# Regrouping a product inside SBUF by small transfers, and moving table building to GpSimd

## Chip, cores and metric

One core of one Trainium2 chip. The time is the device time of one execution in microseconds (us). Every kernel was also executed once under the profiler, and all spans, durations and waits below are from that execution. A time is some 2 us longer than the span of the same execution.

Engines are named as in the profile: PE is TensorE (PEld its weight loads), DVE VectorE, ACT ScalarE, POOL GpSimd, SP SyncE. Here SP only issues transfers.

## The reference, cut to what matters

```python
# A: S = 2048 positions, D = 640 channels
k_shift = sum over t < 4 of k_pad[:, t:t + S, :] * shift_k[:, 3 - t]   # short conv, 4 taps
kv = k_shift * v
y  = irfft(rfft(kv, 2 * S) * rfft(ssm_k, 2 * S))[:S] + kv * ssm_D      # long conv
x  = x + ga * (h * y)                    # h = modulated layernorm of x
# B: gMLP
z  = gelu(h2 @ w_in);  z1, z2 = halves of z
x  = x + gb * ((z1 * (w_sp @ layernorm(z2) + b_sp)) @ w_out)
```

The modulation rows (sa, ca, ga, sb, cb, gb) are silu(c) @ w_mod.

## The kernel before

The long convolution is done as matrix products with cosine tables (M2 forward, G2 inverse), in five units of 128 channels. The operations of part A are recorded with a planned cost and a wish for their time. A planner then takes them one by one, so it fixes the order on each engine, and where it expects PE to stand idle it puts in filler matmuls of the identity. Each engine works its list strictly in order.

The transform wants kv with (8 channels x 16 blocks) on the 128 partitions; the short conv leaves it with one channel to a partition. The kernel before goes through DRAM: one write and one read per unit, 512 KB each.

```python
# tables: "turns" and their rounding; t is the label that the plan orders by
def turns(e):
    new(a, "T", [P, 2, KCH, P], F32)
    for h in range(2):
        e.tensor_scalar(tl[a][:, h], tl["mbase"][:], mstep[:, h * NCH + i:h * NCH + i + 1], MAGIC, op0=ALU.add, op1=ALU.add)
op({"DVE": 540, "POOL": 1000}, turns, ...)
op({"DVE": 650}, lambda e: e.scalar_tensor_tensor(tl[a][:], tl[a][:], MAGIC, ...))   # rounding
# ... Sin on ACT follows

# short conv of unit dt
op({"DVE": 650} if dt == 0 else {"DVE": 650, "POOL": 1050}, diag, ...)    # dg = identity x taps
#   4 times: taps (4 matmuls into PSUM), then times_v: product over v, in place in "big"
op(dma(512, 300), lambda e: e.dma_start(kv_scr[dt * P:(dt + 1) * P, :], tl[name][:, KPAD + S:]), ...)

# per unit, before its first stage: the read
load_X("XU%d" % u, kv_fft, u, ("XU%d" % u, 0), [("kvs", u)])
# kv_fft = kv_scr.rearrange("(c g) (n f) -> (g n) c f", g=8, f=P)
```

## Time and profile before

| kernel before | value | how to read it |
|---|---|---|
| time | 355.31 us | median of 3 runs, 350.15 to 355.49 |
| span | 350.2 us | profiled execution, mean granted clock 0.985 |
| busy | PE 95%, DVE 63%, ACT 40%, POOL 26% | fillers count as busy |
| HBM | read 16.11 MB, written 5.24 MB | includes 5 writes and 5 reads of kv |
| first "pz" (inverse transform) | 52.0 us | end of the ramp |
| first z matmul | 163.0 us | start of part B |

In the profile lines, big holds k and v of a unit and then its product, X the regrouped product or filter, dg the diagonals, T and ZTp the tables of turns, wm a piece of w_mod, Z the result of the inverse transform and ZT its transposed copy; s, sm, pu and pz are results of PE in PSUM.

All later runs of this kernel lie between 350.1 and 355.9 us on one continuous spread. Runs over 1.5% above its fastest count as slow and are left out of the ratios.

One queue of this kernel matters later and is not among the lines that the prediction shows: SP's own timeline (start, duration, queue, line, operation, out<-in). These are the loads of k for units 1 and 2:

```profile
25.71 4.63 SPq L642 DMA_TRANSPOSE big<-in_A_k_dram  x1
...
32.37 1.98 SPq L642 DMA_TRANSPOSE big<-in_A_k_dram  x1
```

Both are issued by 34.4 us, though the product of unit 1 is only written at 45.64 us. In this order SP runs well ahead of need.

### The profile page before, as it was taken

The numbers are of one execution on the slowest core, as the hardware profiler recorded it, in microseconds if no ns is written. First come the engines' busy times: TensorE is split into PE (matmuls) and PEld (weight loads), VectorE is DVE, ScalarE is ACT, GpSimd is POOL, SyncE is SP. The second block draws the span as 40 slices with busy tenths as digits, with TensorE's granted clock in tenths as the row PEclk, the third lists the DMA queues.
The fourth block names the chain that finished last, engine by engine and source line by source line (L and its number), as shares of the span: only waits on it lengthen the run. The fifth ranks groups of instructions, "written<-read, shape, count | busy, mean of one in ns | idle before, by whom it ended". The sixth has DMA issues, their size and how long they took to land.

```text
span 350.2 us, 6998 instructions
## 1 busy us (share of the span) xinstructions
PE 332.2 (95%) x2923; PEld 213.2 (61%) x2929; DVE 219.9 (63%) x465; ACT 139.2 (40%) x225; POOL 89.8 (26%) x101
## 2 busy tenths in 40 slices
PE   8578899999999999998999999999999999999996
PEld 3236458786877988874555555555555555555554
DVE  6887999995857999789787867723223322332323
ACT  2358847878766785536555555200000000000000
POOL 1000310586894796261310023900000000000000
PEclk9789999999999999989999999999999999999999
DMA  7769777993959296430330696057545455631111
GB/s 118 213 194 204 195 206 194 197 250 23 232 89 309 44 249 178 131 97 3 75 75 2 121 216 168 0 113 149 122 107 105 112 126 119 129 87 47 45 45 58
DMA packets 128343, 45.04 MB, mean 129 GB/s; under 512 B 117592, under 2 KB 127672, under 8 KB 128312
## 3 DMA queue, kind: packets, MB, share of 16 engines
q1 hardware_dynamic: 127008, 44.59, 56.4%
q8 instruction: 23, 0.38, 0.4%
q10 hardware_dynamic: 1304, 0.00, 0.2%
q14 instruction: 8, 0.07, 0.1%
HBM read 16.11 MB, written 5.24 MB: 61 GB/s over the span
## 4 chain that ended last, share of the span: by engine, by line
PE 83%; DVE 8%; ACT 5%; issue 2%; POOL 1%; ACTq 0%; DVEq 0%; POOLq 0%
PE ps L1031 27%; PE pz L384 18%; PE pu L384 17%; PE po L1049 9%; PE sm L384 7%; PE s L384 4%; ACT X L406 2%; ACT KH L406 1%; DVE st L692 1%; DVE T L605 1%; DVE st L847 1%; ACT Z L957 1%; DVE T L510 1%; DVE dg L654 1%; DVE T L508 0%
## 5 line engine op out<-in xcount | busy, mean ns | idle before, releaser
L1031 PE MATMUL ps<-X,wT 128*128 128x432 bf16 x512 | 95.7, 346 | 0.0
L1031 PEld LDWEIGHTS <-wT 128*128 128x128 bf16 x512 | 50.1, 98 | 42.2
L605 DVE TENSOR_TENSOR T<-pu,KH 128x1024 bf16<-128x1024 f32 x40 | 47.7, 1218 | 8.1 <-PE pu L384 4.9
L1042 ACT COPY uT<-pt 128x896 bf16<-128x896 bf16 x1 | 0.9, 905 | 118.9 <-PE pt L1041 118.9
L384 PEld LDWEIGHTS <-Z 128*128 128x128 bf16 x320 | 31.2, 98 | 27.4 <-ACT Z L957 0.4
L384 PE MATMUL pu<-X,M 128*128 128x128 bf16 (+1 forms) x480 | 45.4, 237 | 1.1 <-DVE T L605 0.6
L406 ACT CAST X<-s 128x1024 bf16<-128x1024 f32 x40 | 40.9, 1022 | 10.9 <-PE s L384 10.8
L384 PE MATMUL pz<-T,G 128*128 128x128 bf16 (+1 forms) x480 | 41.5, 237 | 0.0
L384 PEld LDWEIGHTS <-M 128*128 128x128 bf16 x480 | 35.8, 98 | 7.3 <-issue 1.3
L1034 DVE SCALAR_TENSOR_TENSOR u<-ps,bcol,G 128x432 bf16<-128x432 f32 x18 | 12.0, 668 | 42.2 <-PE ps L1031 42.2
L384 PEld LDWEIGHTS <-G 128*128 128x128 bf16 x480 | 34.7, 98 | 3.1
L384 PE MATMUL pu<-big,Z 128*128 128x432 bf16 x160 | 33.1, 346 | 0.0
L1049 PE MATMUL po<-w_o,uT 128*128 128x320 bf16 (+1 forms) x224 | 32.8, 299 | 0.0
L384 PE MATMUL pz<-big,Z 128*128 128x432 bf16 x160 | 32.8, 346 | 0.0
L406 ACT CAST Z<-pz 128x512 bf16<-128x512 f32 x40 | 23.5, 592 | 16.8 <-PE pz L384 16.8
L1034 DVE SCALAR_TENSOR_TENSOR u<-ps,bcol,M 128x432 bf16<-128x432 f32 x14 | 9.3, 667 | 30.0 <-PE ps L1031 29.9
L1049 PEld LDWEIGHTS <-uT 128*128 128x128 bf16 (+1 forms) x224 | 21.8, 98 | 9.8
L771 POOL TENSOR_TENSOR gh<-gh,gca_bf 128x512 bf16<-128x512 bf16 x20 | 22.5, 1153 | 18.2 <-DVE gca_bf L758 13.1
L406 ACT CAST KH<-pu 128x512 bf16<-128x512 f32 x40 | 22.7, 600 | 5.9 <-PE pu L384 5.4
L771 POOL TENSOR_TENSOR gh<-gh,gsa_bf 128x512 bf16<-128x512 bf16 x20 | 22.5, 1154 | 7.1 <-DVE gsa_bf L761 7.1
L1051 DVE TENSOR_TENSOR ot<-po,xt 128x320 bf16<-128x320 f32 x32 | 15.7, 492 | 13.4 <-PE po L1049 13.4
L988 DVE BATCH_NORM_STATS2 stz<-X 128x6 f32<-128x432 bf16 x32 | 18.8, 601 | 8.5 <-ACT X L982 8.2
(126 smaller groups left out, 361.0 us busy)
## 6 DMA issues: line engine op xcount, KB each, us to landing
wm<-in_w_mod_dram SPq DMA_DIRECT2D x6, 800.0 KB, 4.9
xt<-in_A_q_dram SPq DMA_DIRECT2D x4, 640.0 KB, 5.5
X<-in_A_ssm_k_dram SPq DMA_DIRECT2D x5, 512.0 KB, 8.0
kv_scr<-big SPq DMA_DIRECT2D x5, 512.0 KB, 3.1
X<-kv_scr SPq DMA_DIRECT2D x5, 512.0 KB, 5.7
out_dram<-ot SPq DMA_DIRECT2D x16, 160.0 KB, 2.2
big<-in_B_w_in_dram SPq DMA_DIRECT2D x2, 1080.0 KB, 6.0
w_o<-in_B_w_out_dram SPq DMA_DIRECT2D x6, 160.0 KB, 3.2
```

What stands on the lines that cost most here:

```text
L384: nc.tensor.matmul(o, lhsT=w, rhs=x, start=start, stop=stop)
L406: (e.copy if e is nc.scalar else e.tensor_copy)(dst, src)
L510: op({"DVE": 650}, lambda e: e.scalar_tensor_tensor(tl[a][:], tl[a][:], MAGIC, tl["mbase"][:, None].to_broadcast([P, 2, KCH, P]), op0=ALU. ...
L605: e.tensor_tensor(T_[:], tl[pu][:, :, :, None, :].to_broadcast([P, KP, 2, 2, DU]), tl[KH][:, :, None, :, :].to_broadcast([P, KP, 2, 2, DU] ...
L654: e.tensor_tensor(tl[dg][:], ident[:, None, :].to_broadcast([P, 4, P]), sk[:, dt, :, None].to_broadcast([P, 4, P]), op=ALU.mult)
L692: e.bn_stats(out=st[:, a, :], in_=xt[:, n, a * HS:(a + 1) * HS])
L771: lambda e, vec=vec, o=o: e.tensor_tensor(gvu, gvu, vec[:, None, d0:d0 + du].to_broadcast([P, TB, du]), op=o),
L988: op({"DVE": 620}, lambda e, i=i, n=n, fc=fc: e.bn_stats(out=stz[:, n, fc, :], in_=tl[z2][:, i, fc * FC:(fc + 1) * FC]), r=[(z2, (i, fc))] ...
L1031: nc.tensor.matmul(ps[:, :FC], lhsT=wTs[t][:, s_, :], rhs=tl["z2_%d" % (s_ // TB)][:, s_ % TB, fc * FC:(fc + 1) * FC], start=(s_ == 0), st ...
L1034: nc.vector.scalar_tensor_tensor(u[:, sl], ps[:, :FC], bcol[:, t:t + 1], z1[t][:, sl], op0=ALU.add, op1=ALU.mult)
L1049: nc.tensor.matmul(ps[:, :HS], lhsT=uTs[t][:fsz[ft], ft, :], rhs=w_o[:fsz[ft], ft, h * HS:(h + 1) * HS], start=(ft == 0), stop=(ft == NFT ...
L1051: nc.vector.tensor_tensor(ot[:, h * HS:(h + 1) * HS], ps[:, :HS], xt[:, t, h * HS:(h + 1) * HS], op=ALU.add)
```

## The change

The intent: drop the DRAM round trip (its latency and its HBM traffic) by 16 transfers per unit from SBUF to SBUF; take the table building off DVE, which is busy in the ramp; load the Sin table of ACT at the start. The planner's wishes were searched again, so the order changed everywhere.

```diff
+        def turn_kv(u):
+            def fn(e):
+                X = new(name, "X", [P, DU // 8, P])
+                for i in range(DU // 8):
+                    e.dma_start(X[:, i, :], tl[kv][i * 8:(i + 1) * 8, KPAD + S:].rearrange("g (n f) -> g n f", f=P))
+            op({"SP": 3700}, fn, ...)
-            op(dma(512, 300), lambda e: e.dma_start(kv_scr[...], tl[name][:, KPAD + S:]), ...)
-            load_X("XU%d" % u, kv_fft, u, ...)
+            turn_kv(u)
-            op({"DVE": 540, "POOL": 1000}, turns, ...)
+            op({"POOL": 1000}, turns, ...)                  # two instructions
-            op({"DVE": 650} if dt == 0 else {"DVE": 650, "POOL": 1050}, diag, ...)
+            op({"POOL": 1050}, diag, ...)
-            op({"DVE": 350, "POOL": 1050}, <negation of a part of G2>)
+            op({"POOL": 1050}, <the same>)
-            op({"DVE": 700}, <copy of a part of G2>)
+            op({"DVE": 700, "ACT": 1040}, <the same>, alt="gc")
+        nc.scalar.activation(warm[:], halfpi[:], ACT.Sin)   # early table load
# cut: f1 and e tables as planned operations, a few planned costs, LOOK 31 -> 94,
# and the tables of wishes WANT, SHIFT, SECOND (all numbers new)
```

On the engines: 16 turns, four diagonals and four negations leave DVE for POOL; six normalizations go from DVE to ACT, three copies of Z from ACT to DVE; 80 transfers stand in place of 10.

## The prediction

> **What bounds the kernel now.** I read the page first, then a table of stretches, then the order of events in the first 60 us, then the groups of the engines that the change touches. On the page I looked at the rows of slices (each slice is 8.75 us):
>
> ```profile
> PE   8578899999999999998999999999999999999996
> ...
> DVE  6887999995857999789787867723223322332323
> ...
> PEclk9789999999999999989999999999999999999999
> ```
>
> TensorE looks busy nearly everywhere, so I asked what it was busy with. The table of stretches gives, after each stretch, its length, then busy us and instruction count of PE, PEld, DVE, ACT and POOL, the granted clock, the DMA share and GB/s:
>
> ```profile
> 10.00:20.00 10.00, 6.55 (x19) 2.35 (x18) 7.76 (x18) 2.72 (x6) 0.00 (x0) 0.66 0.53 140
> 20.00:30.00 10.00, 6.68 (x69) 3.50 (x68) 7.86 (x25) 7.64 (x13) 0.11 (x1) 1.00 1.11 238
> 30.00:40.00 10.00, 9.08 (x110) 6.37 (x108) 9.69 (x28) 9.65 (x16) 0.83 (x2) 1.00 1.08 242
> 40.00:50.00 10.00, 9.66 (x76) 4.59 (x77) 9.12 (x19) 4.87 (x7) 1.87 (x3) 1.00 0.46 151
> 60.00:150.00 90.00, 87.65 (x1243) 73.41 (x1244) 72.19 (x106) 64.22 (x98) 60.24 (x57) 1.00 0.78 169
> ```
>
> Nineteen matmuls in 10 us, then 69, then 110, against 1243 in 90 us later: the early "busy" is partly filler (matmuls of the identity that only keep the clock up) and partly matmuls at a low clock. Both instruction orders contain the same 2853 real matmuls in the recorded part; fillers fall from 76 to 68. So the work on TensorE does not change, and only its waste can. I sized it. By the chain's rows an uninterrupted forward group takes 0.44 us, an inverse group 0.88, a tap group 0.86, and the chain and groups give 0.40 for a first-stage group. 80 x 0.44 + 40 x 0.88 + 20 x 0.86 + 40 x 0.40 is 103.6 us; the modulation, flips and last stage add about 21, so some 124 us. The first z matmul starts at 163.0, after 3 fillers, and from there TensorE is never idle until 340. So about 38 us are waste before 162.5, and nothing after it can change.
>
> Where it lies: the first inverse matmul, "pz", starts at 52.00. Ahead of it in the order stand 12 tap groups, 12 first-stage groups, 12 forward groups, 32 flips and one modulation row: 10.3 + 4.8 + 5.3 + 1.8 + 0.7, about 23 us. So the ramp wastes 29 of the 38 us and the rest 9. The timeline shows why the ramp is slow (start, duration, engine, line, what):
>
> ```profile
> 3.60 1.28 ACT L424 ACT_TABLE_LOAD   x1 [3.60 <-DVE gmask L447]
> ...
> 8.36 1.29 DVE L654 TENSOR_TENSOR dg<-ident,sk 128x512 bf16<-128x512 bf16 x2
> ...
> 13.72 1.28 DVE L669 TENSOR_TENSOR big<-sm,big 128x512 bf16<-128x512 f32 x2
> 14.84 3.62 PE L384 MATMUL sm<-big,dg 128*128 128x512 bf16 x8
> 18.50 0.69 DVE L669 TENSOR_TENSOR big<-sm,big 128x512 bf16<-128x512 f32 x1 [1.01 <-PE sm L384]
> 19.21 0.34 SPq L672 DMA_DIRECT2D kv_scr<-big  x1
> 20.91 0.40 PE L384 MATMUL s<-F1bd,X 64*128 64x128 bf16 x8
> 22.30 0.37 SPq L545 DMA_DIRECT2D X<-kv_scr  x1
> ```
>
> VectorE builds tables first, makes the diagonals at 8.36 and table turns until 13.72; TensorE holds two tap results and waits. Its clock falls, the last two tap groups run at half speed, the product is finished at 19.19, and the kernel's transform starts at 20.91. The ACT copies between its four groups end at 29.7. The regrouped product would have landed at about 28.0 (22.30 plus the median 5.7), yet its first group runs at 31.65: the DRAM trip is mostly hidden behind VectorE and ACT.
>
> **What the Trainium skill says.** "TensorE: Matmul & The Clock Gate", Part 1, has a cold array at half the clock after an idle window of some 3.4 us. The trace agrees: the clock was 0.51 in 15 to 20 us and the two tap groups took 3.62 us instead of 1.72. "DMA: Bandwidth & Descriptors", § Why a DMA increments its semaphore by 16 and not by 1, has a copy use the largest number of engines up to 16 that divides both sides' slowest dimension; a transfer from 8 partitions to 128 would use 8. No run yet shows it. "SBUF — State Buffer", § Who interferes with whom, has a VectorE instruction with two SBUF inputs contend with a GpSimd instruction that reads SBUF; the table rounding that stays on VectorE is of that kind. The trace of before has no such pair close together in the ramp, so it does not say. "ScalarE: Activation LUTs", § What ACT_TABLE_LOAD costs, has about 1283 ns for a load; the row above has 1.28 us.
>
> **The change part by part.** These are the rows whose engine changes (busy us, mean ns; the first five are VectorE from 0 to 60 us):
>
> ```profile
> L669 DVE TENSOR_TENSOR big<-sm,big 128x512 bf16<-128x512 f32 x12 | 7.9, 678 | 2.9 <-PE sm L384 2.9
> ...
> L510 DVE SCALAR_TENSOR_TENSOR T<-T,ZTp 128x512 f32<-128x512 f32 x8 | 5.5, 691 | 0.2
> L508 DVE TENSOR_SCALAR T<-ZTp,mstep 128x256 f32<-128x256 f32 x16 | 4.9, 348 | 0.0
> ...
> L654 DVE TENSOR_TENSOR dg<-ident,sk 128x512 bf16<-128x512 bf16 x4 | 2.7, 684 | 0.0
> ...
> L535 DVE TENSOR_SCALAR G<-G 128x1024 bf16<-128x1024 bf16 x4 | 1.7, 427 | 0.1
> ...
> L654 POOL TENSOR_TENSOR dg<-ident,sk 128x512 bf16<-128x512 bf16 x1 | 1.0, 1040 | 6.8 <-PE sm L384 6.8
> ```
>
> VectorE loses 16 table turns (4.9 us), four diagonals (2.7) and four negations (1.7), all in the ramp, 9.3 us in sum; over the first part it also gives six normalizations of 0.44 to ACT (at 0.92 there) and takes three Z copies of about 0.6. GpSimd, 1.54 us busy in the first 10 us and idle in the next ten, takes 16 turns of about 0.45 (estimate, from 716 ns for its 640-element cast), five diagonals of 1.04 and four negations of about 1.
>
> The Sin table load moves to the start. It lay under VectorE work but held VectorE for 1.0 us before F1bd; gain about 1 us on the way to the first turn.
>
> Transfers: per unit one write and one read of 512 KB go away, 3.1 us and 5.7 us one after the other, 8.8 us. In their place stand 16 transfers of 32 KB. An issue took 338 to 367 ns for either old form, so 16 take about 5.4 us, and the last lands some 2 us later: about 7.4 us. Saved latency 1.4 us a unit; SP is 4.7 us longer in issues but no longer waits for the write to land. HBM loses 2.6 MB each way.
>
> The ramp after, by the new order: 31 fillers before the first tap instead of 22, nine more at about 0.22, so taps start near 10 us (before 9.11). GpSimd has the first four turn pairs at about 6.4 and the diagonal at 7.4, in time. VectorE ends its tables near 8, does four roundings (0.69) and four copies with sign (0.22), and meets the first tap result at about 12.0 instead of 13.72. Tensor idle time there is short, so I expect the clock to hold: four multiplications of 0.68 with tap groups between end at about 15.5, not 19.2. The kernel's transform starts near 15 instead of 20.91; ACT has four copies of 1.02 and eight Sins of 0.46 to do and ends near 22.5 instead of 29.7. The regrouped product lands near 15.5 + 7.4 = 23, just in time. ACT then has the two table loads (3.0), three copies, eight KH copies of 0.58 and three normalizations, to about 38. VectorE's list before the first spectral product is 16.5 us long (eight statistics of 1.1, copies, four multiplications) after about 19: 35.5. So the first "pz" stands at 37 without a stall; I add 3 us for stalls that such a reckoning misses: 40.
>
> In the new order 8 tap groups, 10 first-stage groups, 11 forward groups and the same flips and row stand before it: 6.9 + 4.0 + 4.8 + 2.5, 18.2 us. Its waste is 40 - 18.2 = 21.8 us against 29.0: 7.2 us saved. For the end of this part (9 fillers fall to 4, and gb's product moves ahead) I add 1 us; for the middle, 0. Sum 8.2 us.
>
> **The rivals.** First: the middle gives it back. Work starts earlier but VectorE (72.2 of 90 us), ACT and GpSimd (60.2) still have to serve it, and GpSimd's chain of modulations starts only when w_mod has arrived. For it: GpSimd was at 10.00 of 10 us in one stretch. Against: VectorE's total falls by over 9 us. It would leave 3 to 4 us, a time near 350. Second: GpSimd and VectorE block each other in the first 15 us, and small transfers on half of the engines take 10 us or more; then the product waits at 26 to 28 and the gain is some 4 us. Third: the transfers hardly matter and all of the gain is VectorE relief; this is compatible with my sum, for only 1.4 us of latency is in it. Fourth: the clock. If the longer filler and denser taps avoid every cold window, up to 2 us more come back.
>
> **Range and chances.** The profiled run took 352.19 us for a span of 350.2; the three timed runs average 353.65. Taking 8 to 9 us from these gives 344 to 345.4: I say 344.5. With no stalls (11 us) and a kept clock it is 339 to 341; with the first two rivals 349 to 351. So 339 to 350. Two per cent below the runs of before lies at 346 to 348, a little above my value: faster by over 2% has 0.64, within 2% 0.32, slower by over 2% 0.04.
>
> **What would show it.** Right: from the first z matmul on, the same length as before (187 us); first tap near 10; last multiplication of the first unit at 15 to 16 at full clock; first pz near 37 to 40; the DMA rows of kv_scr gone and 80 issues of about 0.34 us in their place. Wrong: a first pz after 45 (the ramp didn't shorten); a first pz at 38 but z matmuls still after 158 (the middle gave it back, and VectorE or GpSimd is then named in front of the pu and pz groups); low clock in 10 to 25 us; first-stage groups of the product waiting for DMA for over 2 us; roundings on VectorE that take well over 0.69 us beside GpSimd.

## The result and the profile after

The kernel after takes 366.0 us (median of 4 runs, 364.75 to 368.37), beside 353.56 us for the kernel before in the same comparison. The ratio is 1.039 (95% interval 1.028 to 1.051): slower. Ratios here compare fast runs alone, so they are not quite the ratio of the medians. All four runs are of the fast state. The profiled span is 363.0 us, the mean clock 0.972. HBM traffic fell as meant, to 13.49 MB read and 2.62 MB written.

The rows of slices on the page (9.1 us a slice), to set against those of before:

```profile
PE   8387998997999996996999999999999999999996
...
PEclk9977999999999999996899999999999999999999
```

The second slice of PE is a hole now (3, before 5), and the later slices show 7s and 6s where before had 9s. The table of stretches (length, then busy us and count of PE, PEld, DVE, ACT, POOL, then clock, DMA share, GB/s):

```profile
10.00:20.00 10.00, 4.13 (x16) 1.65 (x16) 7.18 (x12) 3.42 (x8) 8.41 (x9) 0.92 0.54 157
20.00:30.00 10.00, 7.24 (x52) 3.50 (x51) 7.94 (x12) 5.26 (x8) 8.29 (x8) 0.67 0.27 36
...
60.00:150.00 90.00, 82.33 (x1127) 66.45 (x1134) 64.17 (x95) 61.02 (x91) 56.87 (x52) 1.00 0.86 176
```

From 10 to 30 us DVE executes 24 instructions in place of 43, and POOL is busy 8.4 and 8.3 of 10 us. From 60 to 150 us PE executes 116 matmuls fewer than before at the same full clock (some records can be missing). So the loss has two places.

The first place, in the timeline (the bracket has the idle time ahead and what ended it):

```profile
2.67 9.01 POOL L502 TENSOR_SCALAR T<-ZTp,mstep 128x256 f32<-128x256 f32 x8 [0.53 <-DVE pj L428]
...
11.64 2.05 POOL L660 TENSOR_TENSOR dg<-ident,sk 128x512 bf16<-128x512 bf16 x2
...
11.72 3.72 DVE L504 SCALAR_TENSOR_TENSOR T<-T,ZTp 128x512 f32<-128x512 f32 x3 [3.92 <-POOL T L502]
...
12.74 1.90 PE L379 MATMUL sm<-big,dg 128*128 128x512 bf16 x8 [2.69 <-POOL dg L660]
```

Eight turns hold POOL for 9 us. The diagonals stand behind them in POOL's list, the first tap waits for a diagonal and starts at 12.74 us (before 9.1), and DVE waits 3.92 us for turns. The summary of single lines (ns: least, median, most) has the sizes:

```profile
L502 POOL TENSOR_SCALAR T<-ZTp,mstep x16: 1137/1148/1509, 2.7 to 23.2; 128x256 f32<-128x256 f32 x16
```

```profile
L504 DVE SCALAR_TENSOR_TENSOR T<-T,ZTp x8: 676/862/2518, 11.7 to 26.2; 128x512 f32<-128x512 f32 x8
```

```profile
L549 SPq DMA_DIRECT2D X<-big x80: 607/607/807, 21.5 to 133.5; - x80
```

A turn is 1.15 us on POOL, against 0.348 on DVE before. The rounding on DVE, 0.691 before, has a median of 0.86 and a longest of 2.52 us. That longest one, at 11.72, lies beside the two diagonals on POOL (11.64 to 13.69), not beside turns: where only turns overlap, roundings take 0.68 to 0.88, and in b_pool, where only the turns moved, 0.96 at most. And an issue of the new transfers is 0.607 us.

The second place, in SP's timeline:

```profile
21.55 10.78 SPq L549 DMA_DIRECT2D X<-big  x16
32.37 1.70 SPq L644 DMA_TRANSPOSE big<-in_A_k_dram  x1
...
45.60 10.41 SPq L549 DMA_DIRECT2D X<-big  x16
56.12 2.02 SPq L644 DMA_TRANSPOSE big<-in_A_k_dram  x1
```

The 16 issues hold SP for 10.4 to 10.8 us a unit, and the loads of k for units 1 and 2 leave only when they are over. PE's waits for transfers between 21 and 175 us (engine, tile and line, what was waited for: us in total, times, longest) are all new; the kernel before had none there:

```profile
PE s L379 <- DMA X<-big: 1.9, 3, 1.2
PE sm L379 <- DMA wm<-in_w_mod_dram: 1.6, 1, 1.6
PE sm L379 <- DMA ZT<-Z: 1.6, 1, 1.6
PE sm L379 <- DMA big<-in_A_k_dram: 1.3, 1, 1.3
```

To compare all kernels I cut each trace at the first pz and at the first z matmul, and reckon for the first two parts the waste: the time, less PE's real work in it at the durations of undisturbed groups. Ahead of the first z stand the same groups in every kernel, 123.4 us of work; 23.0 of it come before the first pz in the order of before and 18.3 in the new order. (Five of the traces lack records of six to nine tap matmuls; the work is counted with them.) Part B has the same work in each kernel, so its plain length stands there. All are profiled executions; an own reckoning, good to some half us.

| kernel | first tap | first pz | waste to first pz | waste first pz to first z | first z to end | span |
|---|---|---|---|---|---|---|
| before | 9.1 | 52.0 | 29.0 | 10.6 | 187.2 | 350.2 |
| after | 12.7 | 49.5 | 31.2 | 18.5 | 189.8 | 363.0 |
| a_both | 10.4 | 43.7 | 25.4 | 11.4 | 189.9 | 350.0 |
| a_turns | 10.3 | 43.9 | 25.6 | 18.9 | 189.5 | 357.4 |
| a_dram | 12.8 | 47.4 | 29.1 | 11.1 | 189.2 | 352.8 |
| b_sbuf | 9.1 | 52.3 | 29.3 | 11.7 | 187.3 | 351.7 |
| b_pool | 9.1 | 56.0 | 33.0 | 10.6 | 187.2 | 354.2 |
| a_hold | 10.3 | 43.9 | 25.6 | 23.0 | 189.0 | 361.0 |
| a_ahead | 10.9 | 43.1 | 24.8 | 17.1 | 189.7 | 355.0 |
| a_nopool | 10.3 | 44.2 | 25.9 | 11.7 | 189.4 | 350.4 |

### The profile page after: what moved, and what is told of

It is laid out like the page before. It is cut to its first block, busy times and chain, and to the rows that moved or that the text cites. A ratio compares the mean times of both kernels' runs of the same rounds, so it can differ in the third digit from the quotient of the medians.

```text
span 363.0 us, 7073 instructions
## 1 busy us (share of the span) xinstructions
PE 333.6 (92%) x2912; PEld 214.2 (59%) x2921; DVE 215.8 (59%) x437; ACT 143.7 (40%) x230; POOL 117.4 (32%) x125
## 3 DMA queue, kind: packets, MB, share of 16 engines
HBM read 13.49 MB, written 2.62 MB: 44 GB/s over the span
## 4 chain that ended last, share of the span: by engine, by line
PE 52%; DVE 6%; ACT 1%; POOL 1%; issue 0%; ACTq 0%; POOLq 0%
PE ps L1036 25%; PE pz L379 9%; PE po L1054 8%; PE pu L379 8%; DVE X L1002 2%; DVE st L851 1%; DVE T L609 1%; ACT Z L962 1%; DVE gh L834 0%; DVE gh L793 0%; POOL xt L845 0%; POOL rstdz L320 0%; PE sm L955 0%; PE pu L816 0%; ACT Z L932 0%
## 5 line engine op out<-in xcount | busy, mean ns | idle before, releaser
L1036 PEld LDWEIGHTS <-wT 128*128 128x128 bf16 x512 | 50.0, 98 | 43.7 <-issue 1.7
L379 PE MATMUL pu<-big,Z 128*128 128x432 bf16 x160 | 34.2, 353 | 0.0
L379 PE MATMUL pz<-big,Z 128*128 128x432 bf16 x160 | 33.6, 348 | 0.0
L401 ACT CAST Z<-pz 128x512 bf16<-128x512 f32 x37 | 21.6, 589 | 18.4 <-PE pz L379 18.4
L379 PE MATMUL sm<-big,dg 128*128 128x512 bf16 x71 | 20.4, 397 | 8.0 <-DVE big L675 3.6
L845 POOL TENSOR_TENSOR xt<-xt,gh 128x512 bf16<-128x512 bf16 x16 | 18.0, 1154 | 22.0 <-DVE gh L793 22.0
```

The source lines that it names most:

```text
L379: nc.tensor.matmul(o, lhsT=w, rhs=x, start=start, stop=stop)
L401: (e.copy if e is nc.scalar else e.tensor_copy)(dst, src)
L845: op(eng, lambda e: e.tensor_tensor(sl, sl, gh[:, g * TB:(g + 1) * TB, d0:d0 + DU], op=ALU.add), r=[("gh", (u, g))], w=[("xt", (u, n)) for ...
L1036: nc.tensor.matmul(ps[:, :FC], lhsT=wTs[t][:, s_, :], rhs=tl["z2_%d" % (s_ // TB)][:, s_ % TB, fc * FC:(fc + 1) * FC], start=(s_ == 0), st ...
```

## The experiments

My theory after the result: two terms were mis-sized, POOL's turns (which lengthens the ramp) and the issues of the transfers (which hold SP, so that the loads behind them come late). The rivals: the new order itself is the loss; the transfers are slow because each takes its data from only 8 partitions; the product's later landing is the loss rather than SP being held. Twelve kernels were run, and the record marks the results of all as correct. That includes a_k16, which is wrong on purpose, so that mark doesn't notice a wrong regrouping. Unless said otherwise, the order on each engine is that of the kernel it was made from.

| kernel | median us (range) | ratio to before, fast runs | 95% interval |
|---|---|---|---|
| a_turns | 360.54 (359.23 to 361.4) | 1.0184 | 1.0118 to 1.025 |
| a_dram | 357.23 (354.61 to 359.93) | 1.0114 | 1.0084 to 1.0145 |
| a_both | 352.27 (350.49 to 355.16) | 0.9988 | 0.9959 to 1.0016 |
| a_k16 | 365.27 (364 to 366.42) | 1.032 | 1.0252 to 1.0388 |
| b_sbuf | 354.06 (351.36 to 355.71) | 1.0011 | 0.9976 to 1.0045 |
| b_pool | 357.21 (355.72 to 358.95) | 1.0096 | 1.007 to 1.0122 |
| a_hold | 363.29 (362.19 to 365.77) | 1.0276 | 1.0202 to 1.0349 |
| a_split | 387.38 (386.99 to 388.47) | 1.0951 | 1.0884 to 1.1019 |
| a_gpq | 381.85 (380.9 to 382.57) | 1.0779 | 1.0728 to 1.083 |
| a_best | 353.75 (351.96 to 355.45) | 1.0014 | 0.999 to 1.0038 |
| a_nopool | 350.48 (349.95 to 352.29) | 0.9886 | 0.9834 to 0.9938 |
| a_ahead | 356.69 (356.05 to 356.87) | 1.0117 | 1.0039 to 1.0195 |

The medians of before in the four calls were 353.26, 354.23, 353.2 and 354.21 us. At 2%, a_k16, a_hold, a_split and a_gpq are slower than before, a_turns and a_ahead unclear, and the others the same.

### a_turns, a_dram, a_both: each part undone alone, and both

a_turns is the kernel after with its turns on DVE:

```diff
             def turns(e):
+                e = nc.vector
```

> The changed kernel with its 16 table turns emitted on VectorE again, everything else and the order on every engine as it is. Theory G (the turns cost 1.15 us each on GpSimd and hold up the diagonals, the first tap and VectorE's roundings): first tap falls from 12.7 to about 10.1, the last multiplication of the first unit from 21.5 to about 18, and the time from 366 to 361 to 363. Theory S (the 16 issues of 0.65 us a unit on SP hold up all later loads, and the ramp only feeds into that wait): first tap falls the same, but the time stays within 2 us, 364 to 366.

a_dram is the kernel after with the product regrouped through DRAM again:

```diff
-                for i in range(DU // 8):
-                    e.dma_start(X[:, i, :], tl[kv][i * 8:(i + 1) * 8, KPAD + S:].rearrange("g (n f) -> g n f", f=P))
+                e.dma_start(kv_scr[u * P:(u + 1) * P, :], tl[kv][:, KPAD + S:])
+                e.dma_start(X[:], kv_fft[:, u * DU // 8:(u + 1) * DU // 8, :])
```

> The changed kernel with the product regrouped through DRAM again (one write, one read, in the place of the 16 transfers), turns still on GpSimd, order as it is. Theory S: SP is held for about 3.5 us a unit instead of 10.4, the first product lands about 9 us after its multiplication instead of 12, later loads come up to 7 us sooner, and the time falls by 5 to 9 us, to 357 to 361. Theory G: the ramp is held by GpSimd, so the time falls by 3 us at most, 363 or more.

a_both has both edits.

> Both undone at once, in the changed kernel's order. If G and S are all of the cause, the waste goes back to that of the kernel before or below and the time is 348 to 355. If a third cause is in it (the new order itself, the diagonals, negations and normalizations that moved), it stays above 357.

a_turns came out just under the range of theory G and a_dram in that of theory S: each part has its share. With both undone the time is that of before (ratio 0.9988). By the medians the transfers cost 360.54 - 352.27 = 8.3 us, the turns 357.23 - 352.27 = 5.0, and both together 13.7, about their sum. In the profiled spans it is 7.4, 2.8 and 13.0; the profiled execution of a_dram is the fastest of its 20. The table of waste shows where each is lost. The turns lie in the ramp (29.1 against 25.4). The transfers lie in the middle (18.9 against 11.4) and take nothing in the ramp as long as the turns are on DVE (25.6 against 25.4); with the turns on POOL the ramp is 2.1 us longer with them (31.2 against 29.1). The rival that the new order itself is the loss falls. With both undone it gains 3.6 us of waste in the ramp and gives back 0.8 in the middle and 2.7 from the first z on, which comes out even.

### a_k16: the same number of transfers, each on all partitions

```diff
-  e.dma_start(X[:, i, :], tl[kv][i * 8:(i + 1) * 8, KPAD + S:].rearrange("g (n f) -> g n f", f=P))
+  e.dma_start(X[:, i, :], tl[kv][:, KPAD + S + i * P:KPAD + S + (i + 1) * P])
```

The result is wrong on purpose: the channels aren't regrouped.

> The changed kernel with the 16 transfers each taking 128 columns of all 128 partitions to the same partitions: same bytes, same 256-byte pieces, same number of issues, and a wrong result on purpose. If an issue of 0.61 us comes from a source that starts with a dimension of 8 (8 engines), it falls to about 0.34 here, 16 take 5.4 us as I had predicted, and the time falls by 3 to 5 us, to 361 to 363. If it comes from the number of issues or the size of pieces, it stays at 0.61 and the time at 364 to 368.

365.27 us, as the kernel after. The issues in the summary of the line:

```profile
L549 SPq DMA_DIRECT2D X<-big x80: 470/599/1602, 17.8 to 134.6; - x80
```

The median is 0.60 us with 128 partitions as with 8. The cost of an issue doesn't come from the narrow source, and a source on all partitions doesn't help.

### b_sbuf, b_pool: each part alone in the order of before

b_sbuf is the kernel before with the write dropped and the 16 transfers in place of the read; b_pool is the kernel before with its turns on POOL.

```diff
 # b_sbuf
-  e.dma_start(kv_scr[dt * P:(dt + 1) * P, :], tl[name][:, KPAD + S:])
+  None
 # in load_X, for kv:
+  for i in range(DU // 8):
+      e.dma_start(X[:, i, :], tl["kv%d" % u][i * 8:(i + 1) * 8, KPAD + S:].rearrange("g (n f) -> g n f", f=P))
 # b_pool, in turns
+  e = nc.gpsimd
```

> The kernel before, in its own order, with only the regrouping changed to the 16 transfers a unit. If the cost of the transfers belongs to them and not to the new order, undoing them gave back 9 us there and putting them in costs 7 to 11 us here: 360 to 364. If it is the new order that put other loads behind them, this one loses less than 4 us, under 357.

> The kernel before, in its own order, with only the 16 table turns emitted on GpSimd. Undoing them in the changed kernel gave back 5.5 us. If their cost belongs to GpSimd's 1.15 us each, the roundings and Sins come late here too: 356 to 360. If the kernel before has room (VectorE starts its roundings only at 10.6 us and GpSimd is idle from 2 us on), it stays within 2 us, 352 to 355.

b_pool loses 0.96%, and the whole of it in the ramp: waste 33.0 against 29.0, so 4.0 us, near the 3.7 of a_dram against a_both in the new order.

b_sbuf loses nothing (ratio 1.0011), though its issues hold SP just as long, at the same median of 0.607 us each. SP's timeline, first unit:

```profile
18.11 10.58 SPq L547 DMA_DIRECT2D X<-big  x16
...
29.23 3.54 SPq L646 DMA_TRANSPOSE big<-in_A_k_dram  x1
```

PE waits for no transfer at all between 21 and 175 us. So it is not the transfers that cost by themselves. In this order the loads have slack: k for units 1 and 2 leaves at 29.23 and 35.59, and the taps of unit 1 come at 40.68 us.

### a_hold: SP held, the product through DRAM

This is a_both with 12 loads of no use after the product's read, so SP is held and the product itself lands as in a_both.

```diff
                 e.dma_start(X[:], kv_fft[...])
+                for i in range(12):
+                    e.dma_start(idle[:, i, :], A_q[0, 0:P, 0:8])
```

> Both undone (352.3 us), and after each read of the regrouped product 12 further small loads that nobody uses, so that SP is held for about 7 us more a unit while the product lands as early as before. If the loss by the transfers is SP being held, and the loads of the next k, v, w_mod behind it, it comes back: 359 to 362. If it is the later landing of the product itself, the time stays at 352 to 354.

SP's timeline, first unit:

```profile
21.05 7.57 SPq L557 DMA_DIRECT2D idle<-in_A_q_dram  x12
28.67 1.70 SPq L652 DMA_TRANSPOSE big<-in_A_k_dram  x1
```

363.29 us, against 352.27 for a_both. PE's waits for transfers from 21 to 175 us are 0.3 us for wm and 0.3 us for the product in a_both. In a_hold the product's stays at 0.3, and there are these:

```profile
PE sm L379 <- DMA ZT<-Z: 3.4, 2, 2.9
...
PE sm L379 <- DMA big<-in_A_k_dram: 2.2, 1, 2.2
...
PE sm L379 <- DMA wm<-in_w_mod_dram: 1.3, 1, 1.3
```

The same three tiles appear as in the kernel after, and the waste lies in the same part (23.0 against 11.4). Holding SP is enough to make the loss, with no transfer of the product changed. It overshoots: the time lies above the expected range, and the span grows by 11.0 us where the transfers cost 7.4. From the write to the last of the 12 loads SP is tied up for 10.6 to 12.3 us a unit, against 10.4 to 10.7 for the transfers in a_turns; that this explains all of the excess is not shown. The later landing falls as the main cause; PE's waits for the product itself in a_turns are 1.5 us, so a small share of it remains possible.

### a_split, a_gpq: other engines issue

Both start from a_turns. In a_split every other transfer is issued by ACT, in a_gpq all by POOL.

```diff
-  e.dma_start(X[:, i, :], ...)
+  (nc.scalar if i % 2 else e).dma_start(X[:, i, :], ...)     # a_split
+  nc.gpsimd.dma_start(X[:, i, :], ...)                       # a_gpq
```

> The changed kernel with the turns on VectorE (360.5 us), and every other of the 16 transfers issued from ACT instead of SP. SP is held for about 5.2 us a unit and the product lands some 5 us sooner; ACT gives 5.2 us a unit to issuing. If the holding of one queue is the loss, 4 to 6 us come back, 354 to 357. If ACT, which has the copies of the ramp to do, or the transfers themselves on 8 engines are the limit, it is 359 or more.

> The changed kernel with its 16 turns on VectorE and with all 16 transfers of a unit issued by GpSimd, which is nearly idle after the tables, in place of SyncE. Theory 1 (the loss of the transfers is SyncE being held, so that the loads behind them come late): SyncE is free as in the kernel with both parts undone, the loads of k and v go out as the product is done, PE waits for no load, and the time comes to 351 to 354 us, against 360.5 with the issues on SyncE. Theory 2 (the transfers cost by themselves, by their number and their small descriptors, whoever issues them): 358 to 362 us. What could spoil theory 1's number: an issue takes longer on GpSimd (over 1 us), so that the product lands later, or the negations and diagonals on GpSimd stand behind them; then the trace shows first stage 1 of the product later than 34 us, and the time lies between.

Both are far slower. a_split lies in its second branch (359 or more), which named ACT's own work or the transfers as the limit. In a_gpq both theories missed: 381.85 us lies outside what either gave, so it doesn't decide between them. In a_split (ACT's timeline) the Sin that follows the issues starts only after them, for they stand in ACT's own list, and stage 1 of the transform waits for ACT:

```profile
18.66 5.87 ACTq L550 DMA_DIRECT2D X<-big  x8
24.57 0.51 ACT L508 ACTIVATE M<-T,mturn 128x256 bf16<-128x256 f32 x1 [4.97 <-DMA X<-big]
```

In a_gpq the issues take about as long (0.64 us median). There is also a second wait: POOL stops between issues until earlier ones have landed, six times for 7.7 us in all.

```profile
19.19 5.52 POOL L550 DMA_DIRECT2D X<-big  x9 [10.68 <-DVE big L676]
25.55 0.59 POOL L550 DMA_DIRECT2D X<-big  x1 [0.84 <-DMA X<-big]
```

POOL also waited 10.68 us for the product with the negations of G2 standing behind. What these two kernels show is that an issue is work in its issuer's list, and that SP, with no other work than issues, was still the cheapest of the three places tried. How a_gpq's loss divides between the stops, the delayed POOL work and late landings stays open.

### a_best, a_nopool: other settings of a_both

a_best has at most 25 fillers in a gap; a_nopool also makes the diagonals and negations on DVE, so nothing that the change moved to POOL stays there.

```diff
 # a_best
-  n, plan.gap = plan.gap if dtype == F32 else 0, 0
+  n, plan.gap = min(plan.gap, 25) if dtype == F32 else 0, 0
 # a_nopool, in the negation and in diag
+  e = nc.vector
```

> Both parts undone, and no more than 25 filler multiplications in a gap in place of up to 31 in the first: a try at a version faster than both kernels. With both undone, the first tap starts at 10.36 us because the fillers end at 10.52, while the diagonals are ready at 8.43; with 25 the first tap can start near 9.0 us. If the chain from the first taps to the first stage 1 sets the ramp: 1 us less, 350.5 to 351.5 us. If the ramp is set by something else (the loads, VectorE's tables): 352 us, the same as without it.

> Both parts undone, and also the diagonals of the short conv and the negations of the tables put on VectorE, so that the changed order stays with nothing of it on GpSimd. If moving these few to GpSimd is what the new order gains (it reaches the first stage 2 with 3.6 us less waste than the kernel before): 354 to 356 us. If the order, not the engine, brings it: 351 to 353 us.

a_best is a miss: the first tap moved from 10.4 to 9.8 us, and the time didn't follow (353.75); the first pz even came later (45.6 against 43.7). a_nopool is the fastest kernel of the study, under both of its expected ranges: 350.48 us, 1.1% below before, within the 2% that counts as the same. Its profiled span equals that of a_both (350.4 and 350.0), so I don't claim a mechanism for the 1.8 us between their medians; its four timed runs had a clock of 0.99, those of a_both 0.971 to 0.99. What it does show is that moving diagonals and negations to POOL bought nothing.

### a_ahead: two loads ahead of the transfers

a_turns with all its transfers, but the loads of k and v for unit 1 stand ahead of the transfers of unit 0 in SP's list, and those for unit 2 ahead of the transfers of unit 1. Only SP's list differs.

```diff
             # in the planner's loop
-            o["fn"](engines[e])
+            if late is not None and (late in o["deps"] or any(g == "X" for _, g in o["new"])):
+                ops[late]["fn"](engines["SP"]); late = None
+            if name in ("XU0", "XU1"):
+                late = i
+                continue
+            o["fn"](engines[e])
+            if late is not None and any(g == "big" for _, g in o["new"]):
+                ops[late]["fn"](engines["SP"]); late = None
```

> The changed kernel with its turns on VectorE, and with one thing moved on SyncE: the loads of k and v for unit 1 stand ahead of the 16 transfers of unit 0, and those for unit 2 ahead of the transfers of unit 1. SyncE is idle from some 10 us until the product of unit 0 is ready, so these loads can go out then. All 80 transfers stay, and SyncE is held by them as long as before. Theory 1 (what the transfers cost in the new order is loads that stand behind them and come late): PE's wait for the load of k (1.0 us with turns on VectorE) goes, and the time falls from 360.5 us to 354 to 357; it does not reach 352.3, since the rows of w_mod and the transposes of ZT (1.9 and 1.6 us of PE's waits) still stand behind transfers. Theory 2 (what costs is the product's own later landing, or the transfers by themselves): 359 to 362 us, no change.

356.69 us, in the range that theory 1 gave. The ratios to before, 1.0117 and 1.0184 for a_turns, have overlapping intervals, but every run of a_ahead (up to 356.87) lies below every run of a_turns (from 359.23), though in another call. The profiled span gets back 2.4 of the 7.4 us of the transfers. SP's timeline shows the load in the time in which SP used to be idle:

```profile
10.02 5.13 SPq L655 DMA_TRANSPOSE big<-in_A_k_dram  x1
...
17.92 10.58 SPq L560 DMA_DIRECT2D X<-big  x16
```

PE's wait for k is gone; of its waits for transfers these are left:

```profile
PE sm L389 <- DMA ZT<-Z: 3.2, 2, 2.0
...
PE sm L389 <- DMA wm<-in_w_mod_dram: 0.8, 1, 0.8
```

The 16th group of pz starts at 86.0 us, against 89.4 in a_turns and 85.6 in a_both. So two loads moved win back nearly all up to there. The rest of the loss (first z at 165.3, against 160.1 in a_both) comes later, where transposes of ZT and rows of w_mod still stand behind the transfers of units 2 to 4. That those are its cause is argued from these waits; I didn't move them.

## Why the prediction was wrong

It said 344.5 us and faster; it is 366 and slower. By its own steps:

- **Same matmuls, only waste can change: right.** The loss is waste, most of it in ramp and middle.
- **"Nothing after it can change": wrong by 2.6 us.** The first z to the end takes 189.8 us, against 187.2. Just ahead of it PE waits 2.5 us for one normalization on DVE, and the clock over the next stretch is low (0.73 from 170 to 180 us, where before 1.00 was granted); later PE waits 1.2 us for DVE's normalization of z2 ahead of the mix. All kernels of the new order have 189.0 to 189.9, those of the old one 187.2 or 187.3, so it belongs to the new order. That the wait brings the low clock was not tested.
- **"16 turns of about 0.45": the first failed step.** 1.15 us each. The estimate scaled from a cast of bf16 out of f32; a two-step operation from f32 to f32 is another thing, and nothing in the profile before had it. The four pairs were done at 11.7 us instead of 6.4, the diagonals at 13.7 (the first in time for 12.74) instead of 7.4, the first unit's last multiplication ended at 21.5 instead of 15.5.
- **The early Sin load: as said.** It runs at 0.72 us, and F1bd no longer waits for it. Its gain of about 1 us was not tested alone.
- **"16 take about 5.4 us": the second failed step.** 0.607 us each, 10.4 to 10.8 us a unit. The 0.34 was read off issues of another form after an idle SP. The profile before had a warning: its issues right behind another took longer (0.43 for xt at 19.60, 0.52 for a load at 55.95). But idle time ahead isn't the whole of it: in the kernel after, the first of each 16 took 0.64 to 0.80 us, also after 11.7 us of idle SP. What sets the 0.607 stays open.
- **"SP is 4.7 us longer in issues but no longer waits": the largest error.** It set SP's holding against the latency of one tile and forgot what stands behind it in the list. b_sbuf (no loss) and a_hold (a larger loss without the transfers) show that the holding, with an order that needs the next load at once, is what costs. "For the middle, 0" thus measured 18.5 - 10.6 = 7.9 us.
- **The relief of DVE as the source of the gain: not borne out.** The first pz was to come at 40; it came at 49.5. Even with both parts undone, the new order reaches it at 43.7, with 3.6 us of waste saved instead of 7.2. Taking diagonals and negations off DVE is worth nothing (a_nopool).
- **The rivals.** The second (blocking, and transfers of 10 us) had the right mechanism in both halves: roundings up to 2.52 us and transfers of 10.4 us. But I made it a smaller gain instead of a loss, since it counted only the product's wait. The first (the middle gives it back) happened by SP, which it didn't name. The fourth brought nothing: the cold stretch only moved (clock 0.92 in 10 to 20 us and 0.67 in 20 to 30, before 0.66 and 1.00).
- **The tests it set.** First tap near 10 (12.74), last multiplication of the first unit at 15 to 16 (21.5), first pz by 40, issues of 0.34, part B of equal length: five failed; kv_scr is gone, as said. Of its signs for "wrong" these came true: first pz after 45, low clock (0.85 and 0.81 in 15 to 25), roundings over 0.69.

The sum in the profiled executions: ramp +2.2 us of waste, middle +7.9, part B +2.6, together 12.7 for a difference of 12.8. Turns cost 3.7 to 5.6 us of the ramp, transfers 7.4 to 7.5 of the middle (and up to 2.1 of the ramp, with the turns on POOL), and the new order alone is even. The planner that made this order had the same two costs too low: its operations carry 1.0 us for a pair of turns (2.3 measured) and 3.7 us for the 16 issues (10.4 measured). Whether a plan made with the measured costs would gain was not tried.

## What to carry to other kernels

An engine that issues transfers is an engine with a list: count issues times their measured duration in the same form, in a row, and ask what stands behind them and how soon it is needed. Replacing one large transfer by 16 small ones saved HBM traffic here and still lost, in the order that needed the next loads soon; in the order with slack it neither lost nor gained. Putting two of the loads ahead of them won back a part of the loss: 2.4 of 7.4 us in the profiled spans, 3.9 of 8.3 by the medians. Before moving an operation to another engine, find a row of that engine for the same operation, type and shape; if there is none, the range has to hold a factor of nearly three, as from 0.45 to 1.15 us here.

## What the Trainium skill lacked or had wrong

- "GPSIMD Engine Reference", § 4.1 Engine selection, has an elementwise operation with one input on GpSimd at roughly line rate and with two inputs about twice slower than on VectorE. Here an addition of two scalars to one 128x256 f32 input took 1.15 us on GpSimd and 0.348 on VectorE, 3.3 times as long. The measurement decides.
- "DMA: Bandwidth & Descriptors", § Anatomy of one DMA — SWDGE (gpsimd) path, gives some 50 ns for the sequencer's dispatch of a transfer issued from GpSimd. In a_gpq such an issue took 0.64 us (median) on POOL. On SP an issue took 0.34 us for a write of 512 KB to DRAM and 0.607 us for 32 KB from SBUF to SBUF.
- The same page, § Issuing engines are not separate DMA queues, calls the issue time usually small relative to the transfer; here 16 issues held SP for 10.4 us, and in the new order the transfers cost 7.4 us of the span. How many engines a transfer from 8 partitions used no run shows; its issue was not the dearer for it (0.60 us with 128 partitions).
- "SBUF — State Buffer", § Who interferes with whom, was right on the contention, but for this case it gives no size: the rounding with two SBUF inputs went from 0.691 to 2.52 us beside two diagonals on GpSimd, and only to 0.96 us at most beside table turns.
- No page that I found says that an issue from GpSimd can stop until earlier ones have landed: 7.7 us in six stops in a_gpq.
